# Infini-attention with a GEGLU block on one core: later set-up memsets, more down work inside the attention phases, the last output projection by groups

## The chip, the core and the metric

The kernel runs on one NeuronCore of a Trainium2 chip. The core has five engines that run their own instruction streams and wait for each other through semaphores: TensorE (PE in the profile; its weight loads are PEld) multiplies matrices into PSUM, VectorE (DVE) and ScalarE (ACT) work elementwise on SBUF and PSUM, GpSimd (POOL) works elementwise on SBUF, and SyncE (SP) issues DMAs. ACT and POOL can issue DMAs too. The metric is the device time of one execution in microseconds.

## What is computed

The input x has 2048 rows of 448. Attention is cut into 4 segments of 512 rows with 16 heads of width 28. In each segment there is causal softmax attention inside the segment and a read of a memory that all earlier segments have written. A gated feed-forward block runs on the same normalised rows, and its SiLU gates the attention's output:

```python
xn = _layernorm(x)
for s in range(N):                       # 4 segments, heads (h), rows (l)
    a_dot = softmax(qs @ ks.T * scale + mask) @ vs
    pq = phi(qs)                         # phi(t) = t + 1 if t > 0 else exp(t)
    a_mem = (pq @ M) / (pq @ z + 1e-6)
    outs.append(g * a_mem + (1.0 - g) * a_dot)
    pk = phi(ks)
    M = M + pk.T @ vs
    z = z + pk.sum()
s = concat(outs) @ wo
g = _silu((_gelu(xn @ w_gate) * (xn @ w_up)) @ w_down)
return x + s * g
```

## The kernel before

The work is staged by segment. A whole segment's normalised rows stand transposed in `xnT` (4 chunks of 128 features by 512 rows). Heads are padded from 28 to 32 columns, so that 4 heads (a group; there are 4 groups) fill 128 partitions; a column of ones in `vaug` lets the product with V deliver the softmax's denominator as well.

The order of the stages is: set-up and `layer_norm_first()` with the projections of segment 0; `gate_up(0)`, `attention(0)`; `gate_up(1)`, `attention(1)`; then `gate_up(2)` and `gate_up(3)` back to back, `attention(2)`, `attention(3)`, and a tail. `gate_up` (L484 to L488) makes 14 blocks of the hidden layer: 8 matmuls, a GELU on ACT, a multiplication on DVE. `attention` (L556 on) has 12 steps, 4 groups by 3 banks of keys, of two half-steps each: score matmuls (L388), exponentials on ACT (L394), masks on POOL (L398), and two steps later the product with V (L409). ACT has about 20 us of exponentials in each attention, so TensorE gets other work in between, the `fill` list: units of a few matmuls each, popped when an estimate of cost says that TensorE is ahead by less than it should be. Such units are the projections of the segment (`project_units`), the down projection (`down_units`, L499: 14 matmuls for each of 4 row blocks, in 5 units; then a tanh on ACT, L502, and a multiply-add on DVE, L506), and the output projection (`finish_units`, L528: 4 matmuls for each row block, a multiplication on DVE, L531, an addition on POOL or DVE, L536 and L539, and the store). `merge` mixes lists evenly by cost; `+` puts one behind another.

The order on each engine is the order of the program; nothing is rescheduled. `later(n, f)` puts a piece off by n ticks of the program's own clock, `flush()` runs all that was put off, and a table (`at`, or the `table` of the tail) names the half-step or unit at which other work is issued.

The softmax is divided out late, and this is what the last part of the change touches. For each group, `evac` (L422, L426) copies the accumulated product from PSUM to SBUF on DVE, and a DMA gathers the rows of denominators into a tile `dc`. `invert` (L440 to L448) scales `dc`, takes reciprocals on DVE, and splits each fp32 value into three bf16 terms (a cast, a subtraction, a cast, a subtraction, a cast: L445 and L447), each written by a DMA into a tile `rows`. `inverses` (L456) multiplies a constant matrix `spread` with the whole of `rows`, which lays the inverse of each head over its 32 partitions in PSUM; `combine` (L468 to L473) and `scale_memory` (L461) multiply it in on DVE. Side 0 of `dc` and `rows` belongs to the attention, side 1 to the memory. Two lines matter:

```python
            r = ps_m.tile([P, L], F32, name="m")
            nc.tensor.matmul(out=r[:], lhsT=spread[:, g, :], rhs=rows[side][:], start=True, stop=True)
```

The matmul reads all rows of `rows[side]`, whichever group it is for, and its result takes one of the three banks of the pool `ps_m`, which the projections, the down and output projections and the memory reads (`memory_read`, L432) share. The scores have a pool of their own, `ps_s` (two tiles of two banks).

At the start (L81 to L160), TensorE runs 145 small matmuls on zeros (L93), while DVE writes constants and the padding of the weights and loads run on SP and ACT. `layer_norm_first` then takes the statistics of the four row blocks (L240, L241, and on POOL L246), scales them (L250), transposes them on TensorE (L260), copies them out on ACT (L261), and projects V in between (L345).

In the tail, `d3[2:]`, 18 units of the down projection of segment 3, is run with a table: the first `invert` (groups 0 to 2) at unit 0, the last two V products at units 1 and 3, `combine` of groups 0, 1 and 2 at units 6, 7 and 8, and the second `invert` (group 3) at unit 8, just ahead of that unit's `combine`. Then come `combine(3, 3)` and the output projection of segment 3.

Of the kernel before, what the change touches and what calls it, by code (L numbers as in the profile page):

```python
# [9 lines left out]
ALU = mybir.AluOpType  # L10
# [7 lines left out]
P = 128  # L18
NSEG = 4
HP = 32  # L20
# [5 lines left out]
def fast_path(tc, A_x, A_wq, A_wk, A_wv, A_wo, A_beta, B_w_gate, B_w_up, B_w_down, out):  # L26
# [16 lines left out]
    with ExitStack() as ctx:  # L43
# [48 lines left out]
        for i in range(145):  # L92
            nc.tensor.matmul(out=idle[:, 0:P], lhsT=wz[:], rhs=wz[:], start=True, stop=True)  # L93
# [24 lines left out]
        def pad_weight(nm):  # L118
            copy = nc.scalar.copy if nm == "wq" else nc.vector.tensor_copy
            copy(out=wpad[nm][:, :, :, 0:Dh], in_=raw[nm][:].rearrange("p c (h d) -> p c h d", d=Dh))  # L120
# [14 lines left out]
        def more_loads():  # L135
            w_dma(nc.sync, wg_sb, B_w_gate)
            w_dma(nc.scalar, wu_sb, B_w_up)
            nc.sync.dma_start(
                out=betac[:],
                in_=A_beta.rearrange("(h o) -> h o", o=1).unsqueeze(1).to_broadcast([H, RC, 1]))  # L140
            load_x(1)
            nc.sync.dma_start(out=wd_sb[:], in_=B_w_down.rearrange("(c p) n -> p c n", p=P))
            wo_v = A_wo.rearrange("(g i d) n -> i d g n", i=HG, d=Dh)
            for i in range(HG):
                nc.sync.dma_start(out=wo_sb[i * HP:i * HP + Dh, :, :], in_=wo_v[i])

        def fill_constants():
            nc.vector.memset(wo_sb[:], 0.0)
            for i in range(2):
                nc.vector.memset(vaug[i][:, :, :, Dh:HP], 0.0)  # L150
                nc.vector.memset(vaug[i][:, :, :, Dh:Dh + 1], 1.0)
# [113 lines left out]
        def layer_norm_first():  # L265
            stats, scale_x, turn = layer_norm(0)
            pad_columns("wq")
            pad_columns("wk")
            fill_constants()
            pad_weight("wq")  # L270
            for b in range(NB):
                stats(b)
            more_loads()
            units0.extend(project_units(0))
            v = units0[8:]
            for b in range(NB):
                scale_x(b)
                turn(b)
                if b:
                    run(v[b - 1:b])  # L280
            pad_weight("wk")
            run(v[NB - 1:])
# [340 lines left out]
        run(units0[:8])  # L623
        check = guard()
# [7 lines left out]
        def tail(s, table, ends, n_inv, n_comb, copy=None):  # L632
            in_turn(table, 0, [ends[0], lambda: ends[1](copy)])
            in_turn(table, n_inv, [lambda: invert(s, 0)])
            return in_turn(table, n_comb, [lambda g=g: combine(s, g) for g in range(G)])

        def memory(s, table, n_read, n_inv, n_scale, copy=None):
            in_turn(table, n_read, [lambda g=g: memory_read(s, g, copy) for g in range(G)])
            in_turn(table, n_inv, [lambda: invert(s, 1)])
# [33 lines left out]
        for s in (2, 3):  # L673
# [3 lines left out]
        ends = attention(2, merge(pu[8:12], pu[:8], finish_units(1)) + d2[:2])  # L677
        at = memory(3, tail(2, {}, ends, 4, 9), 5, 13, 17)
        ends = attention(3, d2[2:] + merge(finish_units(2), d3[:2]), at)
        rest, n = d3[2:], 0  # L680
        fast = dict(eng=nc.vector, queues=[nc.sync, nc.scalar, nc.gpsimd])
        table = {0: [lambda: invert(3, 0, 0, G - 1, nc.vector)], 1: ends[:1], 3: ends[1:],
                 8: [lambda: invert(3, 0, G - 1, G, **fast)]}
        in_turn(table, 6, [lambda g=g: combine(3, g) for g in range(G - 1)])
# [4 lines left out]
        flush()  # L689
        combine(3, G - 1)  # L690
        run(finish_units(3))
        flush()
# [383 lines left out]
```

## Time and profile before

| | us |
|---|---|
| median of 3 runs | 295.4 (294.34 to 296.16) |
| the profiled execution | 295.26 |
| its span, first to last instruction | 293.4 |
| mean granted TensorE clock in it | 0.969 |

The stages in the profiled execution, by the first matmul of each:

| stage | from, us | length, us |
|---|---|---|
| set-up, first normalisation, projections of segment 0 | 0 | 25.4 |
| gate_up(0) | 25.4 | about 28 |
| attention(0), gate_up(1), attention(1) | about 54 | 90.5 |
| gate_up(2), gate_up(3) | 144.5 | 52.7 |
| attention(2) | 197.2 | 28.0 |
| attention(3) | 225.2 | 33.3 |
| tail: down projection, division, output projection | 258.5 | 34.9 |

The last DVE instruction ends at 288.91; the rest of the span is the last store and the program's end. Times in the text are positions in the span, or lengths, in microseconds. A row of a timeline gives start, length, engine, line, operation, the tile written and the tiles read, and in brackets how long the engine had been idle before and what ended that idle time. The rows that carry the argument stand in the prediction.

### The profile page before, as it was taken

How to read it: one execution, taken by the hardware profiler on the slowest of the kernel's cores; microseconds unless marked ns; L12 is line 12 of the kernel's file. 1: busy time of each engine (PE TensorE's matmuls, PEld its weight loads, DVE VectorE, ACT ScalarE, POOL GpSimd, SP SyncE). 2: the span in 40 equal slices, each digit the busy share in tenths (PEclk: the TensorE clock that was granted, in tenths of full speed). 3: DMA queues.
4: the chain of work that ended last, by engine and by line, in shares of the span. 5: the costliest groups of instructions: out<-in, count | busy, mean ns of one | idle time of the engine just before them, and what ended most of it. 6: DMA issues, size and time to landing. Idle time of an engine off the chain costs nothing. (4 is left out here: it accounts for less than half of the span.)

```text
span 293.4 us, 4695 instructions
## 1 busy us (share of the span) xinstructions
PE 261.4 (89%) x1697; PEld 116.9 (40%) x1697; DVE 185.5 (63%) x352; ACT 157.8 (54%) x227; POOL 100.1 (34%) x212
## 2 busy tenths in 40 slices
PE   7789799999999999999999999998999886873770
PEld 7634344433434345444444445443334332231330
DVE  6648666537786787478867654467772585566253
ACT  2338582688985325788853344339896765610000
POOL 4200000145540400976502151304776547550000
PEclk9999999999999999999999999999999998897596
DMA  7997012101010142011110300002000000010002
GB/s 230 349 326 155 19 36 53 49 0 21 19 29 17 29 93 92 12 40 36 35 21 7 72 1 6 7 0 80 17 19 19 4 12 8 32 37 3 2 2 70
DMA packets 26354, 15.11 MB, mean 51 GB/s; under 512 B 17872, under 2 KB 25044, under 8 KB 26324
## 3 DMA queue, kind: packets, MB, share of 16 engines
q1 hardware_dynamic: 23392, 10.20, 14.2%
q10 hardware_dynamic: 2324, 3.16, 3.4%
q0 software_dynamic: 608, 1.38, 1.3%
q8 instruction: 15, 0.25, 0.3%
q14 instruction: 15, 0.12, 0.1%
HBM read 9.18 MB, written 1.84 MB: 38 GB/s over the span
## 5 line engine op out<-in xcount | busy, mean ns | idle before, releaser
L394 ACT ACTIVATE pt<-s 128x1024 bf16<-128x1024 f32 (+1 forms) x96 | 79.3, 886 | 20.1 <-PE s L388 17.9
L398 POOL TENSOR_SCALAR_AFFINE_SELECT pt<-pt 128x256 bf16<-128x256 bf16 x128 | 53.6, 442 | 81.1 <-ACT pt L394 79.6
L487 ACT ACTIVATE gl<-s 128x512 bf16<-128x512 f32 x56 | 33.3, 597 | 58.9 <-PE s L484 41.2
L488 DVE TENSOR_TENSOR hT<-gl,s 128x512 bf16<-128x512 bf16 x56 | 38.5, 687 | 38.1 <-ACT gl L487 37.5
L484 PE MATMUL s<-xnT,wg_sb 128*128 128x512 bf16 x224 | 57.5, 379 | 2.2 <-DVE hT L488 2.2
L484 PE MATMUL s<-xnT,wu_sb 128*128 128x512 bf16 x224 | 57.5, 379 | 0.0
L499 PE MATMUL m<-wd_sb,hT 128*128 128x448 bf16 x224 | 53.9, 375 | 0.0
L484 PEld LDWEIGHTS <-wg_sb 128*128 128x128 bf16 x224 | 21.7, 98 | 28.2 <-issue 3.3
L484 PEld LDWEIGHTS <-wu_sb 128*128 128x128 bf16 x224 | 21.9, 98 | 26.4
L499 PEld LDWEIGHTS <-hT 128*128 128x128 bf16 x224 | 21.4, 102 | 24.4 <-issue 8.5
L388 PE MATMUL s<-qT,kT 32*128 32x512 bf16 (+3 forms) x256 | 22.2, 305 | 3.8 <-ACT pt L394 3.3
L246 POOL TENSOR_TENSOR rstd<-rstd,nhalf 128x2 f32<-128x2 f32 x8 | 5.7, 711 | 50.4 <-DVE rstd L244 50.4
L502 ACT ACTIVATE th<-m 128x448 f32<-128x448 f32 x16 | 8.8, 547 | 25.7 <-PE m L499 25.7
L456 PE MATMUL m<-rows,spread 128*128 128x512 bf16 x28 | 11.5, 417 | 12.2 <-DMA rows<-terms 10.6
L409 PE MATMUL pv<-pt,vaug 128*32 128x512 bf16 (+3 forms) x256 | 17.5, 311 | 0.0
L528 PE MATMUL m<-wo_sb,oT 128*128 128x448 bf16 x64 | 15.0, 355 | 2.3 <-DVE oT L473 1.9
L388 PEld LDWEIGHTS <-kT 32*128 32x128 bf16 x256 | 6.8, 91 | 25.6 <-issue 25.1
L307 PE MATMUL m<-xnT,wq_pad 128*128 128x512 bf16 x64 | 17.0, 380 | 0.0
L307 PE MATMUL m<-xnT,wk_pad 128*128 128x512 bf16 x64 | 16.8, 380 | 0.0
L422 DVE COPY oU<-pv 128x512 f32<-128x512 f32 x14 | 9.6, 684 | 10.4 <-PE pv L409 10.4
L345 PE MATMUL m<-wv_sb,xnT 128*128 128x448 bf16 x64 | 14.7, 353 | 0.6 <-ACT xnT L261 0.5
L311 DVE CAST qT<-m 128x512 bf16<-128x512 f32 x12 | 8.3, 690 | 10.9 <-PE m L307 10.8
(101 smaller groups left out, 291.8 us busy)
## 6 DMA issues: line engine op xcount, KB each, us to landing
x_sb<-in_A_x_dram SPq DMA_DIRECT2D x7, 224.0 KB
wd_sb<-in_B_w_down_dram SPq DMA_DIRECT2D x1, 1568.0 KB
wg_sb<-in_B_w_gate_dram SPq DMA_DIRECT2D x1, 1344.0 KB
wu_sb<-in_B_w_up_dram ACTq DMA_DIRECT2D x1, 1344.0 KB
out_dram<-o_out POOLq DMA_DIRECT2D x12, 112.0 KB, 2.0
xr<-in_A_x_dram ACTq DMA_DIRECT2D x2, 448.0 KB
out_dram<-o_out SPq DMA_DIRECT2D x4, 112.0 KB
wo_sb<-in_A_wo_dram SPq DMA_DIRECT2D x4, 98.0 KB
```

The lines of the kernel that those rows point to most:

```text
L307: nc.tensor.matmul(out=pr[:], lhsT=wpad[nm][:, c, g * HG:(g + 1) * HG, :].rearrange("p h d -> p (h d)"), rhs=xnT[s][:, c, :], start=(c == ...
L345: nc.tensor.matmul(out=vp[:, 0:D], lhsT=xnT[s][:, c, b * P:(b + 1) * P], rhs=wv_sb[:, c, :], start=(c == 0), stop=(c == NDC - 1))
L388: nc.tensor.matmul(out=sp[i // 2][:, i % 2, c0:c0 + n], lhsT=kT[s][r, g, kb * P:(kb + 1) * P], rhs=qT[s][r, g, kb * P:L], start=True, stop ...
L394: nc.scalar.activation(out=pt[:, :, 0:w], in_=sp[pr][:, :, 0:w], func=ACT.Exp, scale=scale)
L398: nc.gpsimd.affine_select(out=v, in_=v, pattern=[[0, 2], [1, P]], compare_op=ALU.is_ge, fill=0.0, base=0, channel_multiplier=-1)
L409: nc.tensor.matmul(out=acc[i * HP:(i + 1) * HP, kb * P:L], lhsT=va[:, kb, g * HG + i, :], rhs=pts[i // 2][:, i % 2, c0:c0 + n], start=(kb ...
L456: nc.tensor.matmul(out=r[:], lhsT=spread[:, g, :], rhs=rows[side][:], start=True, stop=True)
L484: nc.tensor.matmul(out=gu[:, i, :], lhsT=w_sb[:, c, fc * P:(fc + 1) * P], rhs=xnT[s][:, c, :], start=(c == 0), stop=(c == NDC - 1))
L487: nc.scalar.activation(out=gl[:], in_=gu[:, 0, :], func=ACT.Gelu_apprx_tanh)
L488: nc.vector.tensor_tensor(out=hT[s][:, fc, :], in0=gl[:], in1=gu[:, 1, :], op=ALU.mult)
L499: nc.tensor.matmul(out=d_ps[:, 0:D], lhsT=hT[s][:, fc, b * P:(b + 1) * P], rhs=wd_sb[:, fc, :], start=(fc == 0), stop=(fc == NFC - 1))
L528: nc.tensor.matmul(out=a_ps[:, 0:D], lhsT=oT[s][:, g, b * P:(b + 1) * P], rhs=wo_sb[:, g, :], start=(g == 0), stop=(g == G - 1))
```

## The change

At the start: 78 small matmuls instead of 145; the padding of wq moves from ACT to POOL; the load of wo moves from `more_loads` into `fill_constants`; `fill_constants` (memsets for wo, for the padding of w_gate and w_up, for the block mask, `rows` and `spread`) moves from ahead of the statistics to behind the V projections, and the memsets of `vaug` to behind the fourth block's statistics; the V projections come after all four transposes; a `flush()` follows the projections of segment 0.

In attention(2), 8 units of segment 2's down projection are merged in, where 2 stood at the end; attention(3) has the other 12, then 6 of segment 3, and `finish_units(2)` last, no longer merged. The tables change: `invert(2, 0)` at half-step 5 (4 before), its `combine`s from 11 (9); the memory's reads from 1 (5), its `invert` at 8 (13), `scale_memory` from 18 (17). Both inverts split on DVE and not on POOL.

In the tail, 14 down units are left. The first `invert` comes at unit 0 behind the second-last V product, the last V product at unit 1, the second `invert` at unit 6, and `combine` of groups 0 to 2 at units 7, 8 and 9. The output projection of segment 3 no longer goes row block by row block through `ps_m`: it goes group by group into four banks of the scores' pool, so that three groups can be multiplied before the last `combine`. Two of the four last additions go to POOL, and two of the four stores to ACT's queue.

```diff
--- before.py
+++ after.py
@@ -89,7 +89,7 @@
         idle = ps_pv.tile([P, L], F32, name="pv")
         wz = const.tile([P, P], BF16, name="wz")
         nc.gpsimd.memset(wz[:], 0.0)
-        for i in range(145):
+        for i in range(78):
             nc.tensor.matmul(out=idle[:, 0:P], lhsT=wz[:], rhs=wz[:], start=True, stop=True)
         xns = []
         for i in range(2):
@@ -116,7 +116,7 @@
             wpad[nm] = const.tile([P, NDC, H, HP], BF16, name=nm + "_pad")
 
         def pad_weight(nm):
-            copy = nc.scalar.copy if nm == "wq" else nc.vector.tensor_copy
+            copy = nc.gpsimd.tensor_copy if nm == "wq" else nc.vector.tensor_copy
             copy(out=wpad[nm][:, :, :, 0:Dh], in_=raw[nm][:].rearrange("p c (h d) -> p c h d", d=Dh))
 
         def pad_columns(nm):
@@ -140,15 +140,12 @@
                 in_=A_beta.rearrange("(h o) -> h o", o=1).unsqueeze(1).to_broadcast([H, RC, 1]))
             load_x(1)
             nc.sync.dma_start(out=wd_sb[:], in_=B_w_down.rearrange("(c p) n -> p c n", p=P))
+
+        def fill_constants():
+            nc.vector.memset(wo_sb[:], 0.0)
             wo_v = A_wo.rearrange("(g i d) n -> i d g n", i=HG, d=Dh)
             for i in range(HG):
                 nc.sync.dma_start(out=wo_sb[i * HP:i * HP + Dh, :, :], in_=wo_v[i])
-
-        def fill_constants():
-            nc.vector.memset(wo_sb[:], 0.0)
-            for i in range(2):
-                nc.vector.memset(vaug[i][:, :, :, Dh:HP], 0.0)
-                nc.vector.memset(vaug[i][:, :, :, Dh:Dh + 1], 1.0)
             for t in (wg_sb, wu_sb):
                 nc.vector.memset(t[DR:P, NDC - 1, :], 0.0)
             nc.vector.memset(bdmask[:], 0.0)
@@ -266,20 +263,26 @@
             stats, scale_x, turn = layer_norm(0)
             pad_columns("wq")
             pad_columns("wk")
-            fill_constants()
-            pad_weight("wq")
-            for b in range(NB):
+            for b in range(3):
                 stats(b)
             more_loads()
+            pad_weight("wq")
+            scale_x(0)
+            turn(0)
+            scale_x(1)
+            turn(1)
+            stats(3)
+            for i in range(2):
+                nc.vector.memset(vaug[i][:, :, :, Dh:HP], 0.0)
+                nc.vector.memset(vaug[i][:, :, :, Dh:Dh + 1], 1.0)
+            scale_x(2)
+            turn(2)
+            scale_x(3)
+            turn(3)
+            pad_weight("wk")
             units0.extend(project_units(0))
-            v = units0[8:]
-            for b in range(NB):
-                scale_x(b)
-                turn(b)
-                if b:
-                    run(v[b - 1:b])
-            pad_weight("wk")
-            run(v[NB - 1:])
+            run(units0[8:])
+            fill_constants()
 
         def layer_norm_steps(s, table):
 
@@ -621,6 +624,7 @@
         units0 = []
         layer_norm_first()
         run(units0[:8])
+        flush()
         check = guard()
 
         def phase(s, table):
@@ -629,14 +633,14 @@
             if s + 2 < NSEG:
                 load_x(s + 2)
 
-        def tail(s, table, ends, n_inv, n_comb, copy=None):
+        def tail(s, table, ends, n_inv, n_comb, copy=None, eng=None):
             in_turn(table, 0, [ends[0], lambda: ends[1](copy)])
-            in_turn(table, n_inv, [lambda: invert(s, 0)])
+            in_turn(table, n_inv, [lambda: invert(s, 0, eng=eng)])
             return in_turn(table, n_comb, [lambda g=g: combine(s, g) for g in range(G)])
 
-        def memory(s, table, n_read, n_inv, n_scale, copy=None):
+        def memory(s, table, n_read, n_inv, n_scale, copy=None, eng=None):
             in_turn(table, n_read, [lambda g=g: memory_read(s, g, copy) for g in range(G)])
-            in_turn(table, n_inv, [lambda: invert(s, 1)])
+            in_turn(table, n_inv, [lambda: invert(s, 1, eng=eng)])
             return in_turn(table, n_scale, [lambda g=g: scale_memory(s, g) for g in range(G)])
 
 
@@ -674,22 +678,38 @@
             xr[s] = x_sb[s]
         ok = nc.values_load(oki[0:1, 0:1], min_val=0, max_val=1)
         pu, d2, d3 = project_units(3), down_units(2), down_units(3)
-        ends = attention(2, merge(pu[8:12], pu[:8], finish_units(1)) + d2[:2])
-        at = memory(3, tail(2, {}, ends, 4, 9), 5, 13, 17)
-        ends = attention(3, d2[2:] + merge(finish_units(2), d3[:2]), at)
-        rest, n = d3[2:], 0
-        fast = dict(eng=nc.vector, queues=[nc.sync, nc.scalar, nc.gpsimd])
-        table = {0: [lambda: invert(3, 0, 0, G - 1, nc.vector)], 1: ends[:1], 3: ends[1:],
-                 8: [lambda: invert(3, 0, G - 1, G, **fast)]}
-        in_turn(table, 6, [lambda g=g: combine(3, g) for g in range(G - 1)])
+        ends = attention(2, merge(pu[8:12], pu[:8], finish_units(1), d2[:8]))
+        at = memory(3, tail(2, {}, ends, 5, 11, eng=nc.vector), 1, 8, 18, eng=nc.vector)
+        ends = attention(3, d2[8:] + d3[:6] + finish_units(2), at)
+
+        v = dict(eng=nc.vector, queues=[nc.sync, nc.scalar, nc.sync])
+        table = {0: [ends[0], lambda: invert(3, 0, 0, G - 1, **v)], 1: ends[1:],
+                 6: [lambda: invert(3, 0, G - 1, G, **v)],
+                 7: [lambda: combine(3, 0)], 8: [lambda: combine(3, 1)], 9: [lambda: combine(3, 2)]}
+        rest = d3[6:]
         for n, u in enumerate(rest):
             run([u])
             for f in table.get(n, ()):
                 f()
         flush()
+        acc = [ps_s.tile([P, 2, L], F32, name="s") for _ in range(2)]
+
+        def wo_part(g):
+            for b in range(NB):
+                nc.tensor.matmul(out=acc[b // 2][:, b % 2, 0:D], lhsT=oT[3][:, g, b * P:(b + 1) * P],
+                                 rhs=wo_sb[:, g, :], start=(g == 0), stop=(g == G - 1))
+
+        for g in range(G - 1):
+            wo_part(g)
         combine(3, G - 1)
-        run(finish_units(3))
-        flush()
+        wo_part(G - 1)
+        for b in range(NB):
+            t = sg.pop((3, b))
+            nc.vector.tensor_tensor(out=t, in0=t, in1=acc[b // 2][:, b % 2, 0:D], op=ALU.mult)
+            o_out = outp.tile([P, D], BF16, name="o_out")
+            add = nc.vector if b % 2 else nc.gpsimd
+            add.tensor_tensor(out=o_out[:], in0=t, in1=xr[3][:, b, :], op=ALU.add)
+            (nc.scalar if b % 2 else nc.sync).dma_start(out=o_v[3][:, b, :], in_=o_out[:])
         return ok
 
 
```

## The prediction

> **What bounds the kernel now.** I read the page's slices first, then busy time by stage, then the list of waits, then the timeline of the start and of the end. TensorE is busy 89% of the span, so the question is where it isn't, or is slow:
>
> ```profile
> span 293.4 us, 4695 instructions
> ...
> PE 261.4 (89%) x1697; PEld 116.9 (40%) x1697; DVE 185.5 (63%) x352; ACT 157.8 (54%) x227; POOL 100.1 (34%) x212
> ...
> PEclk9999999999999999999999999999999998897596
> ```
>
> Full clock (9) until slice 36, then a falling clock: the loss sits at the end. By stage (columns: window, its length, PE, PEld, DVE, ACT, POOL busy with counts, granted clock, DMA share, GB/s), attention(1), attention(2), attention(3), then two stretches of the tail:
>
> ```profile
> 112.00:144.50 32.50, 32.50 (x254) 14.14 (x253) 23.61 (x39) 26.29 (x36) 20.36 (x39) 1.00 0.15 39
> ...
> 197.20:225.20 28.00, 26.03 (x196) 9.78 (x194) 17.81 (x28) 23.50 (x30) 18.50 (x40) 1.00 0.11 35
> 225.20:258.50 33.30, 27.64 (x211) 10.35 (x210) 19.65 (x34) 21.32 (x28) 19.47 (x46) 0.95 0.05 13
> 258.50:273.10 14.60, 6.31 (x34) 2.31 (x33) 9.01 (x20) 1.09 (x2) 3.25 (x6) 0.83 0.07 20
> 273.10:283.40 10.30, 8.49 (x30) 3.58 (x30) 3.88 (x6) 1.09 (x2) 0.00 (x0) 0.74 0.00 2
> ```
>
> Attention(1) is TensorE without a gap. Attention(2) follows ScalarE (23.5 of 28.0); attention(3) is longer, with less on ScalarE: nothing is full, so it is waits. They are these (engine, line, what it waited for: total, times, longest):
>
> ```profile
> PE m L456 <- DMA rows<-terms: 10.6, 4, 5.7
> ...
> PE s L388 <- ACT pt L394: 3.3, 10, 0.6
> ...
> PE s L484 <- DVE hT L488: 2.2, 3, 1.8
> ```
>
> and in the timeline of the tail (start, us, engine, line):
>
> ```profile
> 258.94 1.69 DVE L445 CAST terms<-dc 96x64 bf16<-96x64 f32 x1
> ...
> 264.63 0.52 PE L456 MATMUL m<-rows,spread 128*128 128x512 bf16 x1 [2.63 <-DMA rows<-terms]
> ...
> 271.29 0.64 POOL L448 DMA_DIRECT2D rows<-terms  x1 [9.87 <-issue]
> ...
> 273.11 0.61 PE L456 MATMUL m<-rows,spread 128*128 128x512 bf16 x1 [5.67 <-DMA rows<-terms]
> ...
> 273.50 7.31 PE L499 MATMUL m<-wd_sb,hT 128*128 128x448 bf16 x25
> ```
>
> The reader is to see two round trips in a row, each ending in a wait, and 25 down matmuls that then take 0.29 us each, not 0.19: the clock has dropped. The second wait arises because `combine(3, 2)` is issued after the second `invert` and reads all of `rows`.
>
> **The change, part by part.** Sums are against the profiled execution, 295.26 us with a span of 293.4; the runs' median is 295.4, so 0.14 is added at the end and lost in rounding.
>
> *Start.* Before, statistics begin at 7.48, the q/k projections at 18.50, `gate_up(0)` at 25.40. Of DVE's set-up only what ends at 2.23 stays ahead. x (448 KB, first on both queues) must be there by about 4.2: the core moved 285 GB/s from 2 to 4 us and 369 from 4 to 6 (estimate). Two statistics at 0.70 and the sum 0.2 end at 5.8, the `pow` on POOL (0.72) at 6.5, blocks 0 and 1 are scaled (0.39 each) by 7.4. The wq padding moves from ACT (1.69) to POOL. No such copy runs there before; the nearest row is POOL's cast of 128x512 at 0.61, so 1792 elements are 2.1 us, bounds 1.7 (ACT's row) and 3. wq lands at 6.94 (ACT's wait for it ended there), so POOL is taken until 9.05; behind it is queued the second `pow`, for it blocks 2 and 3 wait: 9.8, then scaling, transposes, V from 11.2 to 14.3 (16 matmuls, 0.19 each), not 18.5.
> A row speaks against it: the 1.69 us cast above began on DVE, and ended at 260.63, just as POOL's 1.03 us addition ended (260.56); the same cast on 32 rows took 0.19. The Trainium skill (SBUF — State Buffer, "SBUF: two separate sides") says that a DVE instruction in a two-port mode and a GpSimd instruction lock each other out for the whole instruction. If scaling falls under it, the POOL copy holds block 1 up until 9.05 and V ends at 15.9; if not, 14.3. I can't tell from 0.39 us which mode it runs in; I take the middle.
> Then `fill_constants` stands on DVE in front of the k evacuations: the same memsets took 3.9 us before (0.81 x 3, 0.11, 0.47, 0.55, gaps). With three m banks, the fifth q/k unit waits for the first k evacuation: 1.9 us given back. `gate_up(0)` starts at 23.2 to 24.8. The wo loads wait on SP for a memset at about 16 us, ahead of the pkb transposes (23.8 before), which nobody needs before `update(0)` at 55: nothing. The wg/wu loads no longer follow the padding memsets: ready earlier. The added `flush()` puts the last phi exponentials ahead of the first GELU, so two table loads (27.95 and 29.89, 1.28 each) go, and the 1.81 us that TensorE waited for hT at 32.55; a first GELU behind one load still costs 0.7, so 1.1 is gained.
> The other rule is about the clock. 78 dummy matmuls (about 35 at 0.1, then 0.056 us) end at 7.5, and until V starts TensorE has only transposes (0.4 each). The skill (TensorE: Matmul & The Clock Gate, "Part 1") drops the clock after an idle window of about 3.4 us; by that nothing happens. In the trace it dropped at 247.7 after a stretch with 1.1 us of work in 3.4. By the row V could run at half speed (+1.7); by the rule, 0. I take the rule's 0 here, since V begins inside the window, and keep 1.7 for the range.
> Start: -2.0 (from -4.5 to +1).
>
> *Attention(2)* gets 17 more down matmuls (8 units, not 2), 3.2 us. By the yardstick of attention(1), 32.5 us less its update (1.05) and 50 down matmuls (9.5), TensorE needed 22.0 of the 28.0 us; ScalarE, with 23.5, was the bound. The cover is 6 us of TensorE's slack; ScalarE gets one tanh, 0.55. +0.7; without the cover +3.2.
>
> *Attention(3)*: `memory_read` goes from half-step 5 to 1, its `invert` from 13 to 8, `scale_memory` from 17 to 18: ten half-steps to hide the `rows` round trip, not four. Before, TensorE waited 2.06 us at 247.73, then ran at clock 0.5 for 3.4 us, and ScalarE was starved (3.65 and 1.97 idle). From 245.67 to 254.25 it did 3.9 us of matmuls at full-speed spacing in 8.6: 4.7 goes. `combine` of segment 2 waits two more half-steps: of the 2.2 lost at 235.4 to 241 perhaps 1.0 goes, the rest being waits for m banks. Six down matmuls fewer: 1.1. The splits move to DVE, 5 x 0.2 us per invert, on an engine with 13.7 us free here; the hop to POOL and back (0.70) goes. Late next is POOL: the four finishes stand in the last five half-steps, 1.03 + 0.3 + 0.56 each, among eight masks at 0.44, 11 us where about 7 pass; the last pv waits for a mask. 0.3 in this stage. -6.5 (from -3.8, the row wait and clock alone, to -9.4, ScalarE's 22.6 plus 1.3).
>
> *Tail*, from T, the end of the loop (258.5 before; the end lies at T+34.9). 11 down matmuls went; but now the second `invert` stands ahead of all `combine`s, so one long chain: first invert at T+1.2, 2.1 long (row 268.49 to 270.56); the evacuation of the last group behind it on DVE, 0.7; dc by DMA 1.9 (229.21 to 231.11); second invert 2.1; `rows` 1.8: T+9.8, and 0.7 for one POOL addition in the way: `combine(3, 0)` at T+10.5. TensorE is done at T+5.0 (23 x 0.19 and pv) and waits 5.5. Then 16 down matmuls and 3 inverses: 3.7 at full clock, 7.2 at half; one window or two are slow, 6.0: T+16.5. wo of three groups, 12 x 0.19: T+18.8. Inverse and two DVE instructions, 1.8: T+20.6; last group 0.4; six DVE instructions at 0.64 (two of eight go to POOL): T+24.9. From there 4.5, as before (288.91 to 293.4), and 0.5 for POOL's additions meeting DVE's: T+29.9. -5.0 (from -7 to -2).
>
> Sum: -2.0 + 0.7 - 6.5 - 5.0 = -12.8: 282.5.
>
> **Rivals.** *Filled elsewhere* (0.18): attention(2) pays its 3.2 in full, attention(3) gets 3.8, the tail 4, the start 0: -4.6, about 290.5. For it: attention(2) runs near ScalarE's floor. Against: 6 us of free TensorE.
> *The set-up doesn't do what it says* (0.15, inside the forecast's 0.60): copy, memsets and clock eat the earlier statistics, start +0: 284.5.
> *m banks* (0.07, slower): down accumulators are parked in one of three m banks through both phases, so 32 other uses (12 projections, 4 finishes; 4 reads, 8 inverses, 4 finishes) share two, and each may wait for its DVE evacuation, 0.69 + 0.2. Above 0.49 us a use the gain is gone and 1% with it; at 0.6 it is 19.2 - 12.8: 301.7. For it: TensorE waited 2.0 us on DVE for banks in attention(3) before, 0.17 a use. Against: attention(1) parks a down accumulator throughout and has no gap.
>
> **How the numbers follow.** Forecast (277 to 287) 0.60; more, if both phases reach ScalarE's floor and the clock holds, 0.09; filled elsewhere (287 to 292.4) 0.18; within 1%, which is about what a measurement of this kernel can tell from none, 0.06; slower 0.07. Faster by over 1%: 0.87. 275 to 291 leaves out some 0.03 below and 0.17 above.
>
> **What would show it.** Statistics at 4 to 5 us; gate_up(0) at 23 to 25 with no 1.8 us wait for hT; attention(2) 28 to 29.5 us; attention(3) 26 to 28 with no wait for rows; in the tail one wait for rows of 4 to 6 us, and a drop of the clock after it. Wrong if attention(3) stays above 30, if `m` waits on DVE grow beyond 10 us, or if the statistics still start at 7.

## The result and the profile after

The changed kernel takes 287.24 us (median of 4 runs, 285.97 to 289.29), the kernel before in the same comparison 295.78: a ratio of 0.971, with a 95% interval from 0.963 to 0.980. That is 8.5 us less, inside the stated range of 275 to 291, but two thirds of the 12.8 us that were forecast, and 0.2 us above the band of 277 to 287 that was given 0.60.

From the page of the changed kernel:

```profile
span 285.6 us, 4547 instructions
...
PE 255.9 (90%) x1630; PEld 113.3 (40%) x1630; DVE 190.8 (67%) x360; ACT 153.7 (54%) x224; POOL 100.8 (35%) x204
...
PEclk9889999999999999999999999999999999999795
```

Counted from 0, the clock was reduced before in slices 33 and 34 (attention(3)), which the prediction read as full, and in 36, 37 and 39 (the tail). Now it is reduced in two of the tail's, 37 and 39, and there is a new dip at the start, in slices 1 and 2. By stage (window, length, busy time of PE, PEld, DVE, ACT and POOL, clock, DMA share, GB/s): attention(2), attention(3), then the tail in two stretches, up to the first `combine` and up to the last group's output projection.

```profile
196.70:226.10 29.40, 28.54 (x215) 11.12 (x214) 19.80 (x29) 24.44 (x32) 18.16 (x39) 1.00 0.09 30
226.10:253.80 27.70, 24.12 (x200) 9.11 (x200) 20.92 (x41) 20.61 (x28) 15.38 (x36) 1.00 0.07 19
253.80:265.40 11.60, 5.61 (x36) 2.37 (x34) 7.46 (x17) 1.06 (x3) 4.26 (x8) 0.99 0.09 25
265.40:275.40 10.00, 8.44 (x35) 3.75 (x36) 6.49 (x10) 1.09 (x2) 0.00 (x0) 0.84 0.01 2
```

Attention(2) grew to 29.4 us, with TensorE busy in 28.5 of them: it took the work. Attention(3) shrank to 27.7, at full clock throughout. The wait for `rows` that it had before, first row, is gone, second row, and what TensorE waits for `rows` in the whole span has halved, third row:

```profile
247.73 0.59 PE L456 MATMUL m<-rows,spread 128*128 128x512 bf16 x1 [2.06 <-DMA rows<-terms]
```

```profile
247.06 0.39 PE L459 MATMUL m<-rows,spread 128*128 128x512 bf16 x1
```

```profile
PE m L459 <- DMA rows<-terms: 5.2, 2, 5.0
```

The timeline of the start (start, us, engine, line, what; in brackets the idle time before and what ended it):

```profile
6.62 2.19 DVE L247 TENSOR_SCALAR xn<-x_sb,mv,rstd 128x448 bf16<-128x448 bf16 x2
...
7.00 1.67 POOL L120 COPY wq_pad<-oT 128x1792 bf16<-128x1792 bf16 x1 [0.42 <-DMA oT<-in_A_wq_dram]
...
12.23 4.87 PE L348 MATMUL m<-wv_sb,xnT 128*128 128x448 bf16 x16
...
22.64 1.02 PE L310 MATMUL m<-xnT,wk_pad 128*128 128x512 bf16 x4 [1.22 <-DVE kT L314]
...
29.78 1.02 PE L487 MATMUL s<-xnT,wg_sb 128*128 128x512 bf16 x4 [0.93 <-DVE hT L491]
```

The statistics do start at 4.01, not 7.48. But the two scalings took 2.19 us together where one takes 0.39: the second ended at 8.81, just behind POOL's copy (8.67). The scalings of blocks 2 and 3 took 0.56 and 0.88 us, and each also ended 0.13 us behind an instruction of POOL (at 11.14 and 11.94). The V projections took 4.87 us, 0.3 us each, at a mean clock of 0.64. `gate_up(0)` starts at 25.23, 0.17 earlier than before. The timeline of the tail:

```profile
256.08 1.82 DVE L450 TENSOR_TENSOR dc<-dc,terms 96x64 f32<-96x64 f32 x1
...
256.52 0.64 PE L412 MATMUL pv<-pt,vaug 128*32 128x256 bf16 x4 [1.00 <-POOL pt L401]
256.78 1.03 POOL L542 TENSOR_TENSOR o_out<-sg,x_sb 128x448 bf16<-128x448 f32 x1
...
265.45 0.58 PE L459 MATMUL m<-rows,spread 128*128 128x512 bf16 x1 [4.97 <-DMA rows<-terms]
...
272.93 0.38 PE L459 MATMUL m<-rows,spread 128*128 128x512 bf16 x1
...
274.82 0.93 PE L699 MATMUL s<-wo_sb,oT 128*128 128x448 bf16 x4 [1.51 <-DVE oT L476]
```

One wait for `rows` of 5.0 us stands where there were two, of 2.6 and 5.7. A subtraction of the first `invert` took 1.82 us, not 0.22, and ended with an addition on POOL. The last `combine` (272.93) comes behind the output projection of three groups.

Where attention(3) ends has to be settled before the stages are compared. The tail begins with the first down matmul that stands behind the loop. The kernel before has 50 of them there (18 units), the changed kernel 39 (14 units); counted back from the last one, they begin with these rows, the first of before, the second of the changed kernel:

```profile
257.29 1.30 PE L499 MATMUL m<-wd_sb,hT 128*128 128x448 bf16 x6
```

```profile
253.78 0.73 PE L502 MATMUL m<-wd_sb,hT 128*128 128x448 bf16 x3
```

The 258.5 that the table of before and the prediction took is the first V product of the tail, two units later. Attention(3) of before was thus 32.0 us long and its tail 36.1, not 33.3 and 34.9. From the two profiled executions (spans 293.4 and 285.6):

| stage | forecast | measured |
|---|---|---|
| start and gate_up(0), to the first V of attention(0) | -2.0 | -1.0 (53.25 to 52.21) |
| attention(0) to gate_up(3) | 0 | +0.4 |
| attention(2), to the first scores of attention(3) | +0.7 | +1.5 (27.9 to 29.4) |
| attention(3) | -6.5 | -4.3 (32.0 to 27.7) |
| tail | -5.0 | -4.3 (36.1 to 31.8) |
| sum (before rounding) | -12.8 | -7.8 |

### The profile page after: what moved, and what is told of

Read it like the earlier page. It is cut to its first block, busy times and chain, and to the rows that moved or that the text cites. A ratio compares the mean times of both kernels' runs of the same rounds, so it can differ in the third digit from the quotient of the medians.

```text
span 285.6 us, 4547 instructions
## 1 busy us (share of the span) xinstructions
PE 255.9 (90%) x1630; PEld 113.3 (40%) x1630; DVE 190.8 (67%) x360; ACT 153.7 (54%) x224; POOL 100.8 (35%) x204
## 4 chain that ended last, share of the span: by engine, by line
PE 59%; issue 11%; ACT 9%; DVE 7%; POOL 7%; DMA 5%; SPq 0%; ACTq 0%; POOLq 0%; DVEq 0%
PE s L487 28%; PE m L502 10%; ACT pt L397 5%; PE m L310 5%; PE s L391 4%; PE m L348 4%; PE pv L412 3%; POOL o_out L542 2%; POOL pt L401 2%; DMA oT<-in_A_wq_dram 2%; DMA xnT<-xn 1%; PE m L459 1%; PE m L531 1%; ACT gl L490 1%; ACT ph_e L326 1%
## 5 line engine op out<-in xcount | busy, mean ns | idle before, releaser
L490 ACT ACTIVATE gl<-s 128x512 bf16<-128x512 f32 x56 | 33.3, 597 | 60.2 <-PE s L487 45.3
L502 PE MATMUL m<-wd_sb,hT 128*128 128x448 bf16 x224 | 51.8, 359 | 0.2 <-DVE sg L509 0.2
L502 PEld LDWEIGHTS <-hT 128*128 128x128 bf16 x224 | 20.4, 99 | 22.7 <-issue 5.7
L391 PE MATMUL s<-qT,kT 32*128 32x512 bf16 (+3 forms) x256 | 21.2, 301 | 2.1 <-ACT pt L397 1.8
L459 PE MATMUL m<-rows,spread 128*128 128x512 bf16 x28 | 10.9, 405 | 5.6 <-DMA rows<-terms 5.2
L348 PE MATMUL m<-wv_sb,xnT 128*128 128x448 bf16 x64 | 15.5, 386 | 0.2 <-DVE vaug L350 0.2
L335 DVE SCALAR_TENSOR_TENSOR pqT<-qT,ph_e 128x512 bf16<-128x512 bf16 x12 | 12.4, 1032 | 0.4
```

Of the source, the lines that this page charges most:

```text
L335: nc.vector.scalar_tensor_tensor(out=ph, in0=dst[:, g, :], scalar=1.0, in1=e[:], op0=ALU.add, op1=ALU.max)
L348: nc.tensor.matmul(out=vp[:, 0:D], lhsT=xnT[s][:, c, b * P:(b + 1) * P], rhs=wv_sb[:, c, :], start=(c == 0), stop=(c == NDC - 1))
L391: nc.tensor.matmul(out=sp[i // 2][:, i % 2, c0:c0 + n], lhsT=kT[s][r, g, kb * P:(kb + 1) * P], rhs=qT[s][r, g, kb * P:L], start=True, stop ...
L490: nc.scalar.activation(out=gl[:], in_=gu[:, 0, :], func=ACT.Gelu_apprx_tanh)
L502: nc.tensor.matmul(out=d_ps[:, 0:D], lhsT=hT[s][:, fc, b * P:(b + 1) * P], rhs=wd_sb[:, fc, :], start=(fc == 0), stop=(fc == NFC - 1))
```

## The experiments

Every kernel below was timed in three rounds beside the kernel before. The interval of such a ratio is about ±0.4 to 1%, so 1.5 us between two of them is at the edge of what the medians can tell; where the text decides on less, it does so by profiles, and says so. One length is of use throughout: the tail, from the first down matmul behind the loop. Five profiles have the changed kernel's tail without an edit to it (the changed kernel, the start undone, the tables undone, more small matmuls, the memsets moved), and it is 31.8, 32.9, 33.8, 32.5 and 32.8 us long in them. An edit of the tail is visible in one profile only if it leads out of that range.

**The start undone.**

```diff
-        for i in range(78):
+        for i in range(145):
-            copy = nc.gpsimd.tensor_copy if nm == "wq" else nc.vector.tensor_copy
+            copy = nc.scalar.copy if nm == "wq" else nc.vector.tensor_copy
...
-            for b in range(3):
+            fill_constants()
+            pad_weight("wq")
+            for b in range(NB):
...
+            v = units0[8:]
+            for b in range(NB):
+                scale_x(b)
+                turn(b)
+                if b:
+                    run(v[b - 1:b])
             pad_weight("wk")
-            run(units0[8:])
-            fill_constants()
+            run(v[NB - 1:])
...
-        flush()
```

> The changed kernel with the start of the kernel before (145 small matmuls, wq padded on ACT, all constants ahead of the statistics, V between the transposes, no flush). Theory from the two traces: the start is worth 1.0 us in all, 0.2 up to the first matmul of gate_up(0) and 0.9 in gate_up(0) itself; so this run ends about 1 us later than the changed kernel, 288.2, its four V blocks take 0.8 us each again and the first wait for hT is 1.8. Rival (the sum of the prediction): the start is worth 2.0, so 289.2. Second rival: what the start gives is lost later anyway, 287.2.

289.58 us, ratio 0.985 (0.979 to 0.991). V took 0.9 us a block and the wait for hT was 1.81 again. That is 2.3 us above the changed kernel, though the two intervals touch. By the profiles, `gate_up(1)` begins at 84.16 here and, in the eight profiles with the changed start, at 80.5 to 82.9, with a median of 82.3. So the start is worth something, and rather 2 us than 1; the profile of the changed kernel, with 82.85, was the latest of the eight. Which of the start's parts gave it isn't separated.

**The tables of attention(3) undone**, with the moved down work left in place.

```diff
-        at = memory(3, tail(2, {}, ends, 5, 11, eng=nc.vector), 1, 8, 18, eng=nc.vector)
+        at = memory(3, tail(2, {}, ends, 4, 9), 5, 13, 17)
```

> The changed kernel with the tables of the kernel before in attention(3): invert(2,0) at 4, its combines from 9, memory reads from 5, their invert at 13, scale_memory from 17, splits on POOL; the fill lists stay as changed. Theory: the schedule of the memory's round trip is what shortened attention(3), so the wait for rows of about 2 us and the half clock after it return there: attention(3) 31 to 32 us, not 27.7, and 291 in all. Rival: it is the moved down work that did it, and attention(3) stays under 28.5: 287.5 to 288.

292.03 us, ratio 0.988 (0.983 to 0.993), 4.8 us above the changed kernel. Its attention(2) and attention(3) by stage, and its waits in attention(3):

```profile
195.90:225.30 29.40, 28.53 (x213) 11.13 (x210) 19.83 (x29) 24.38 (x32) 18.15 (x39) 1.00 0.09 30
225.30:257.40 32.10, 26.75 (x201) 9.48 (x201) 18.93 (x32) 20.95 (x28) 18.25 (x45) 0.89 0.07 17
```

```profile
PE m L459 <- DMA rows<-terms: 2.2, 2, 2.1
```

The wait and the reduced clock (0.89) are back. Attention(2) is the same to 0.1 us. Its loop ends at 257.17, so attention(3) is 31.8 us long against 27.7: of the 4.3 us by which it became shorter, this line accounts for 4.1. The six down matmuls that left the stage can have given little beside it, 0.2 us in these profiles; the mean clock is lower here than before (0.89, not 0.95), so a part of what they gave may be hidden. The line holds several things at once: when the memory is read, inverted and scaled, when segment 2 is inverted and combined, and that the splits run on DVE. The returning wait points to the first, but no run separates them. Together they are worth about half of the whole change.

**The tail's order undone**, on its 14 units.

```diff
+        fast = dict(eng=nc.vector, queues=[nc.sync, nc.scalar, nc.gpsimd])
+        table = {0: [lambda: invert(3, 0, 0, G - 1, nc.vector)], 1: ends[:1], 3: ends[1:],
+                 8: [lambda: invert(3, 0, G - 1, G, **fast)]}
+        in_turn(table, 6, [lambda g=g: combine(3, g) for g in range(G - 1)])
...
+        combine(3, G - 1)
+        run(finish_units(3))
```

> The changed kernel with the tail's order of the kernel before on its 14 down units: last V products at units 1 and 3, combines at 6, 7, 8, the second invert just ahead of the third combine, output projection by row blocks through the m banks, all additions on DVE. Theory: the two waits for rows return (2 to 3 us and 5 to 6 us), but the four down units that went are still gone, so the tail is 32.5 to 33.5 us long, not 31.8: 288 to 289. Rival: the single chain is what pays, and the tail goes back to 34.9: 290.3.

287.62 us, ratio 0.974 (0.969 to 0.979). Both waits are back, as its timeline shows:

```profile
260.96 0.38 PE L459 MATMUL m<-rows,spread 128*128 128x512 bf16 x1 [2.15 <-DMA rows<-terms]
...
268.70 0.61 PE L459 MATMUL m<-rows,spread 128*128 128x512 bf16 x1 [5.41 <-DMA rows<-terms]
...
269.11 4.14 PE L502 MATMUL m<-wd_sb,hT 128*128 128x448 bf16 x14
```

and still the time is that of the changed kernel, within what can be measured: the tail is 32.4 us long, from 253.6 to 286.0, inside the range of the five. The two short chains cost what the one long chain costs, as far as a spread of 2 us lets one see. The old order with 18 units took 36.1, so what the change gained in the tail is the four units, eleven matmuls, that left it. Most of it falls in the stretch behind the second wait, where 25 down matmuls took 7.31 us and 14 now take 4.14.

**The end undone alone**: `combine(3, 3)`, then the output projection by row blocks.

```diff
-        for g in range(G - 1):
-            wo_part(g)
         combine(3, G - 1)
-        wo_part(G - 1)
...
+        run(finish_units(3))
+        flush()
```

> The changed kernel with only the end undone: combine(3,3), then the output projection by row blocks, additions and stores on DVE and SP. Theory from the trace: by groups the 12 matmuls of three groups stand ahead of the last inverse and delay it by 2.3 us, which is as much as they save behind it, so the end moves by less than 0.7 us either way: 286.6 to 287.9. Rival: the projection by groups takes 12 matmuls (2.3 us) off the end, and this run is 2 us longer: 289.2.

285.55 us, ratio 0.966 (0.963 to 0.970), 1.7 us below the changed kernel, and so not what either theory said. The intervals overlap, so this is not certain; but nothing supports that the output projection by groups takes 2 us off the end: the tail is 31.1 us long here, below all five with an unedited tail. In the profile of this run:

```profile
271.84 0.38 PE L459 MATMUL m<-rows,spread 128*128 128x512 bf16 x1
...
274.68 2.63 PE L531 MATMUL m<-wo_sb,oT 128*128 128x448 bf16 x13 [1.89 <-DVE oT L476]
```

the last inverse comes 2.8 us before the last group's projection starts, where it came 1.9 before in the changed kernel. DVE's last addition ends at 280.10, the changed kernel's at 280.04; from there it is 4.6 us to the end, not 5.5. The next two runs ask for these two.

**The last combine first.**

```diff
+        combine(3, G - 1)
         for g in range(G - 1):
             wo_part(g)
-        combine(3, G - 1)
         wo_part(G - 1)
```

> The changed kernel with combine(3,3) ahead of the 12 wo matmuls of the first three groups, not behind them. Theory: the last inverse stands 2.3 us earlier on TensorE, DVE then waits for its last tanh and multiply-add, so the last group's wo starts 1.2 us earlier: 286. Rival: the clock or the tanh decides and nothing moves: 287.2.

285.60 us, ratio 0.966 (0.956 to 0.976). TensorE's wait for the last oT fell from 1.51 to 0.19 us: that the wait is gone is shown. Its worth is not. The tail is 32.0 us long, inside the range of the five, and the last group's projection starts 20.8 us after the loop and not 21.0, for the 11 down matmuls ahead of it took 3.38 us, where they took 2.28 in the changed kernel's profile. The start's clock was full in this profile, so a part of the 1.6 us in the median may come from there.

**The last additions on DVE, the last stores on SP.**

```diff
-            add = nc.vector if b % 2 else nc.gpsimd
-            add.tensor_tensor(out=o_out[:], ...)
-            (nc.scalar if b % 2 else nc.sync).dma_start(...)
+            nc.vector.tensor_tensor(out=o_out[:], ...)
+            nc.sync.dma_start(...)
```

> The changed kernel with all four last additions on DVE and all four last stores on SP. Theory: the span ends 5.6 us after DVE's last addition with the last store on ACT's queue, 4.5 to 4.6 with it on SP (the kernel before, and the run with the end undone), so 1.0 is gained there; DVE has two additions more (1.3) but no longer waits 0.34 and 0.72 for POOL: together -0.7 (286.5). Rival: the two engines and two queues do shorten the end, by 1.3: 288.5.

288.18 us, ratio 0.975 (0.967 to 0.983): a miss. From the last addition (281.35) to the end it was 5.0 us, so 0.6 was gained, not 1.0, and DVE's eight instructions took 5.0 us, where six with POOL's help had taken 4.6. The medians show no gain, and no loss beyond the interval. All profiles together lean to a small gain: from DVE's first multiplication of the end to the end of the span it is 10.0 to 11.1 us in the eight with both engines and both queues, and 9.5 to 10.4 in the six with DVE and SP alone (three of these project by row blocks).

**More small matmuls between the transposes.**

```diff
             scale_x(1)
             turn(1)
+            for i in range(30):
+                nc.tensor.matmul(out=idle[:, 0:P], lhsT=wz[:], rhs=wz[:], start=True, stop=True)
```

> The changed kernel with 30 more small matmuls on zeros (1.7 us at full clock) between the second and the third transposes. Theory: TensorE's 1.9 us of idleness there is what dropped the clock, and the V projections then took 4.87 us; filled, they take 3.1 to 3.3, the V evacuations and the memsets behind them on DVE move up with them, and gate_up(0) starts 1.4 to 1.8 us earlier: 285.5 to 286. Rival: DVE with its memsets is the bound of the start, V gets faster but the wait for the first k evacuation grows by as much: 287.2.

285.56 us, ratio 0.967 (0.959 to 0.974), and `gate_up(0)` at 22.82, 2.4 us earlier. The stretch ahead of V and V itself, first in the changed kernel, then in this run:

```profile
8.70:12.10 3.40, 0.89 (x10) 0.56 (x11) 2.88 (x11) 1.30 (x3) 2.11 (x4) 1.00 1.02 405
12.20:16.90 4.70, 4.70 (x20) 2.11 (x18) 2.03 (x4) 0.60 (x2) 1.58 (x2) 0.64 1.06 300
```

```profile
8.50:11.50 3.00, 2.45 (x41) 2.10 (x39) 2.55 (x8) 1.63 (x3) 2.75 (x5) 1.00 1.02 403
11.50:14.60 3.10, 3.10 (x21) 1.64 (x18) 2.12 (x4) 0.58 (x1) 1.56 (x2) 1.00 1.04 367
```

With 0.89 us of work in 3.4 the clock fell to a mean of 0.64 in V; with 2.45 in 3.0 it stayed. One profile could be chance, for V also stays at full clock without the matmuls in some executions. In the run with the last `combine` first, which has the changed kernel's start, it did so behind a stretch as empty as the one above:

```profile
8.40:11.80 3.40, 0.90 (x14) 0.56 (x12) 2.92 (x9) 1.66 (x3) 3.15 (x5) 1.00 1.01 393
```

```profile
11.82 3.19 PE L348 MATMUL m<-wv_sb,xnT 128*128 128x448 bf16 x16
```

With the 30 matmuls V took 3.19 us in all three profiles that have them (this one and the two of the last section). Without them it took 3.19 in three of nine and 4.5 to 4.9 in six. That the matmuls keep the clock up is thus likely, but not certain. The wait for the first k evacuation is still 1.22 us: DVE moved up along with V, and was not the bound.

**The memsets moved once more**: the padding of w_gate and w_up into the time in which DVE waits for x (1.78 us), the rest into `gate_up(0)`.

```diff
...
+            for t in (wg_sb, wu_sb):
+                nc.vector.memset(t[DR:P, NDC - 1, :], 0.0)
             for b in range(3):
                 stats(b)
...
-            fill_constants()
...
         layer_norm_steps(1, table)
+        in_turn(table, 10, [fill_constants])
```

> The changed kernel with the memsets moved once more: the padding of w_gate and w_up into DVE's free time ahead of the first statistics, the rest of fill_constants (with the load of wo) into gate_up(0). V stays at half clock. Theory: the 1.22 us that TensorE waits for the first k evacuation goes, and part of the wait for hT (0.93), for phi is earlier too: 285 to 286. Rival: it waits elsewhere for as long: 287.2.

285.53 us, ratio 0.967 (0.959 to 0.975). The wait of 1.22 us is gone, the wait for hT is 0.62, and `gate_up(0)` starts at 21.12. V happened to run at full clock in this profile, without any matmul added, so its start can be compared with that of the run before: 1.7 us earlier than 22.82.

**A tile of its own for the last group's inverses.**

```diff
+        rows.append(const.tile([P, L], BF16, name="macc"))
+        nc.vector.memset(rows[2][:], 0.0)
...
-                 6: [lambda: invert(3, 0, G - 1, G, **v)],
+                 6: [lambda: invert(3, 0, G - 1, G, row=2, **v)],
...
-        combine(3, G - 1)
+        combine(3, G - 1, 2)
```

> The changed kernel with a tile of its own for the last group's inverses, so that combine(3,0..2) reads rows that only the first invert wrote. Theory: the 5.0 us wait in the tail is for the second invert, which these three groups don't need; with it go the wait but for 1 us and the half clock behind it, and the tail becomes 5 to 7 us shorter: 280.5 to 282.5. Rival: the last group's own chain sets the end (its rows come 8.9 us after the last V product, whatever the others do), and less than 2 us is gained: 285.5.

285.36 us, ratio 0.967 (0.962 to 0.973): the rival's size, but not for the rival's reason. In its timeline the wait for `rows` is gone, and a new one stands behind it:

```profile
258.40 0.38 PE L459 MATMUL m<-rows,spread 128*128 128x512 bf16 x1 [0.29 <-issue]
...
259.05 0.25 DVE L443 TENSOR_SCALAR dc<-dc,igate 32x64 f32<-32x64 f32 x1 [0.57 <-DMA dc<-oU]
...
261.10 0.69 DVE L475 TENSOR_TENSOR oU<-oU,m 128x512 f32<-128x512 f32 x1
...
261.84 0.73 PE L502 MATMUL m<-wd_sb,hT 128*128 128x448 bf16 x3 [2.47 <-DVE oU L475]
...
263.55 3.45 PE L502 MATMUL m<-wd_sb,hT 128*128 128x448 bf16 x11
```

The first inverse is ready at 258.4, but the second `invert` stands ahead of `combine` on DVE: it waits for its DMA and then takes 2 us, and only at 261.10 does DVE read the inverse out of its bank. TensorE finds none of the three banks free and stands still for 2.5 us; the clock falls again (11 matmuls in 3.45 us). The wait moved from a DMA to DVE's queue. The tail is 30.7 us long, so it did gain 1 to 3 us against the five, not the 5 to 7 of the theory; V ran at full clock in this profile, so the time of the whole says less. Putting the second `invert` behind the `combine`s as well wasn't tried.

**Segment 2's last additions off POOL.**

```diff
-                    if s == NSEG - 1:
+                    if s >= NSEG - 2:
                         nc.vector.tensor_tensor(out=o_out[:], in0=t, in1=xr[s][:, b, :], op=ALU.add)
                         nc.sync.dma_start(out=o_v[s][:, b, :], in_=o_out[:])
```

> The changed kernel with segment 2's four last additions on DVE and their stores on SP, not on POOL. Theory: POOL's additions hold up the last mask (TensorE waited 1.0 us for it) and one DVE subtraction of the first invert (1.82 us, not 0.22); without them the wait for rows ends about 1.5 us earlier after the end of the loop: 285.7. Rival: four additions more on DVE and four stores ahead of dc and rows on SP's queue cost as much: 287.2.

285.60 us, ratio 0.966 (0.961 to 0.971). In the profile the last V product no longer waits for a mask, the subtraction takes 0.22 us, and the wait for `rows` ends 10.1 us after the loop (254.03 to 264.16), not 11.7. One wait of TensorE for a bank in attention(3) grew from 0.85 to 1.48, and that stage is 28.5 us long, not 27.7, while the tail is 30.3: the holds by POOL are shown, and a part of what their end gives is lost again ahead of the tail.

**Together.** The rows tile, the small matmuls, the memsets, the last combine first, and additions and stores at the end on DVE and SP, though no gain was shown for the last; then the same with segment 2's additions off POOL.

> All that seems to pay together: the rows tile of its own, the 30 small matmuls, the memsets moved once more, the last combine ahead of the wo matmuls, last additions on DVE and stores on SP. Theory: the start and the tail add up, -2.5 to -3.5 at the start, -5 to -7 in the tail: 277 to 280. Rival: they share a bound, DVE at the end or the loads at the start, and it stays above 281.

> The one before with segment 2's last additions and stores off POOL too. Theory: with the long wait gone, the mask and the first invert are what the tail waits for, and 1 to 1.5 us more is gained: 276 to 279. Rival: DVE is full at the end of attention(3), and it is 0.5 us or more slower than the one before.

281.56 us, ratio 0.952 (0.947 to 0.957), and 279.44 us, ratio 0.946 (0.941 to 0.951). The first misses its range (277 to 280) by 1.6 us and lies where the rival put it, above 281. In its profile the start gave 4.1 us (attention(2) begins at 192.6, not 196.7), more than expected, and the tail, 30.3 us and so 1.5 shorter, much less: TensorE still waits 1.9 us for DVE to free a bank. The second misses its range (276 to 279) by 0.4; it adds 2.1 to the first, more than the 1 to 1.5 expected, though the two intervals overlap. Both are clearly below the changed kernel's 0.963 to 0.980.

## Why the prediction came out as it did

The direction, and where most of the gain lies, were right: attention(3) and the tail gave 4.3 us each in the profiles, and undoing the one line of attention(3) takes 4.8 us back. The gain was two thirds of the forecast. By its steps:

- *Start, -2.0 forecast.* The parts named there add up to -2.5 (`gate_up(0)` at 24.0, the middle of 23.2 to 24.8, is 1.4 earlier, and 1.1 for hT); the text doesn't say where the other 0.5 went. The early statistics (4.0 to 5.8) came as worked out, and the case that the text feared came: the scaling of block 1 had to wait for POOL's copy (1.67 us long; 2.1 was taken). The step that failed is the clock. The text had a row for it (a stretch with 1.1 us of work in 3.4 after which the clock dropped), weighed a rule against it, and took the rule's 0. In the changed kernel's profile the row was right: 0.89 us of work in 3.4, and V at 4.87 us, not 3.1, +1.75 against the +1.7 that the row gave. But the row isn't a rule either. In the eight profiles with this start, V took 3.19 us in two and 4.5 to 4.9 in six, and `gate_up(1)` started at 80.5 and 80.8 or at 82.1 to 82.9. The median, 82.3, is 1.65 us earlier than the 83.90 of before, so that -2.0 came out nearly right although the clock had been put at nothing. That is luck in part: the wait of the next point had been taken 0.7 too high, and 0.5 of the gain had been left out of the sum. The Trainium skill (TensorE: Matmul & The Clock Gate, "Part 1") calls the window over which the clock is decided free-running, which fits the eight profiles; none of them shows the window itself.
- *The wait for the first k evacuation* was put at 1.9 and was 1.22; the wait for hT was to gain 1.1 and gained 0.9.
- *Attention(2), +0.7.* It was +1.5, the same in every profile. That TensorE had 6 us of slack was too much: its own row of before has it busy in 26.0 of 28.0, which leaves 2.0, and it is now at 28.5 of 29.4. What ScalarE does in the stage grew by tanhs alone, 0.55 us each. Which of the two sets the length now, no run shows.
- *Attention(3), -6.5.* It was -4.3. The main item, 4.7 for the row wait, its clock and what follows, is close to the 4.1 that undoing the line gave back. What failed are the smaller items, 1.0 for the later `combine` and 1.1 for the six down matmuls: beside the main item 0.2 us are left in the profiles. POOL was late next, as named, at a higher price: the last V product waited 1.0 us for its mask. That falls into the tail.
- *Tail, -5.0.* It was -4.3, and the nearness is luck. The text put the end at T+29.9 and it came at T+31.8; but it also put the end of before at T+34.9, where from the same point it was T+36.1. The first `combine` came 11.7 us after the loop and not 10.5, for POOL's addition held a DVE subtraction up by 1.6 us and not 0.7; the six instructions at the end took 4.6 us and not 3.8, as POOL's additions stood in DVE's way; the end came 5.5 us behind them, where 5.0 was taken with that contention in it. And the sum leaves more to the new order than it gave: eleven matmuls at 0.19 to 0.29 us are 2.1 to 3.2 of the 5.0, the rest was to come from one chain for two and from the end by groups. With the old order on the same 14 units the time is the same within what can be measured, and with the old end it is not longer.
- *The rivals.* "Filled elsewhere" was half right: attention(2) paid more than forecast and attention(3) gave 4.3, near its 3.8, but the start gave something and the tail 4.3. "m banks" fell: in attention(3) TensorE waited 2.5 us in all for DVE to free a bank, 0.15 us a use for 16 uses, where 0.49 was the point from which it decides. "The set-up doesn't do what it says" is near the truth in those executions in which the clock drops.

What stays open is how much the output projection by groups costs: the profile without it shows an earlier inverse, a shorter end and a tail 0.7 us below the shortest of the five, but the medians' intervals overlap.

## What to carry to other kernels

Where a small value goes through a DMA and back, give it more of the program's steps before anything reads it, ahead of making its chain shorter: here ten half-steps between the memory's `invert` and its first use, where there were four, with what else that line holds, were worth 4 to 5 us, and a merged chain in the tail nothing that could be measured. When a wait is taken away, look at the queue of the engine that reads the result: the wait for `rows` came back as a wait behind an `invert` on DVE. And where the trace shows the clock fall after a merely sparse stretch, don't put that at nothing, and don't count on it either: here it came in six of nine executions, so the forecast should carry it as a chance. Before two kernels are compared by stage, fix the boundary by counting the same instructions in both.

## What was not expected of the hardware

The same instructions differ by up to 2.4 us at the start (`gate_up(1)` at 80.5 to 82.9), and by about 1.3 at the end, from one execution to the next, with the clock: V took 3.19 or 4.87 us, and the 11 down matmuls ahead of the last output projection took from 2.24 to 3.54 us in the five profiles that share their tail. A stretch with 0.90 us of matmuls in 3.4 was followed by full clock once, one with 0.89 by a mean of 0.64. A profile's single figure for such a stage is a draw, and the stage has to be read from several.

POOL and DVE met in several places, and there DVE's instruction ended shortly behind POOL's, however long that was. A scaling of 0.39 us took 1.88 beside the copy, and three scalings in the start each ended 0.13 us behind an instruction of POOL. A subtraction took 1.82 us, not 0.22, and ended 0.09 behind POOL's addition; with segment 2's additions off POOL it took 0.22 again, so there the cause is shown. An addition at the end took 0.97, not 0.63, and ended 0.49 behind POOL's. It isn't so for every pair: the multiplications at the end, which read PSUM, kept their 0.61 us beside POOL's additions.
